# Output projection of a gated mix of attention and feed-forward: seven products for two tiles of results

## The chip, the cores and the metric

The kernel runs on one core of a Trainium2 chip. TensorE multiplies matrices (a stationary operand of 128x128 is loaded, then a moving one streams through), VectorE (DVE), ScalarE (ACT) and GpSimd (POOL) work element by element, SyncE (SP) issues the transfers. Results of TensorE land in PSUM, in eight banks of 512 f32 numbers per partition. Each engine runs its own list of instructions in order, and they wait for each other by semaphores. The metric is the device time of the whole program in microseconds.

## The reference

```python
def _A_ref(x, wq, wk, wv, wo, beta):      # 32 heads of 18, segments of 512 tokens
    ...                                   # local softmax and a memory of earlier segments
    return o @ wo                         # the output projection: [2048, 576] x [576, 576]

def _B_ref(x, w_gate, w_up, w_down):
    return (_gelu(x @ w_gate) * (x @ w_up)) @ w_down      # 576 -> 4608 -> 576

g = _sigmoid((x * gate_w).sum(-1, keepdims=True))
return g * _A_ref(x, ...) + (1 - g) * _B_ref(x, ...)
```

All arrays are f32. The output is [1, 2048, 576].

## The kernel before

Every f32 operand of a large product is scaled by a power of two and split in two f16 words, a high half (rounded) and a low half (what the rounding left). A product of two such operands takes three f16 products: high x high, high x low, low x high. A scale is made from a sum of squares, by a product with a matrix of ones (`sums`, L91, through `scale_sum`) and a few tiny operations of VectorE (L98 to L101). `low_x` (L175) makes the low half of x, `pair_high` and `pair_low` (L109, L112) the halves of a weight.

The program has three parts. First come the projections to q, k and v, with the memory of the attention (to 219.6 us). Then `step(v)` runs for v = 0 to 71, two steps for each of 36 slices of 128 hidden columns of the feed-forward part. A step makes gate and up for 1024 tokens (`product`, `rest`, `low_rests`; they already use a form with seven products for two by two blocks, whose sums of weights GpSimd makes), a share of the attention, and a share of the down projection of earlier slices (`chains`, `down`). The halves of the hidden values are made by `hidden` (VectorE, L1029) and `hidden_pair` (ScalarE L1033, GpSimd L1034). `end_pair` does this at the beginning of the next step for the products that a step left open. Third, behind the last step, come the last block of `down`, 16 tiles of 128 tokens with two halves of 288 columns each (32 chains of six products), and the output projection.

In the output projection the rows of the attention's result, tile t of 128 tokens, are loaded back and transposed by transfers (`turned(t)`, into `ot[t]`: four high tiles of 128 columns, four low ones, and one that holds both halves of the last 64 columns). W_o is loaded and squared by `finish(0)` and `finish(1)` behind steps 69 and 70, scaled by `finish(2)`, and its halves are made by `finish(3)` and `pair_low`. Each of 32 results (tile t, half n) takes 14 products (`chain_x`, L332 to L335): three for each of four tiles of columns and two for the last. VectorE then multiplies by the gate and adds to `acc` (L1327), and SP stores the tile.

The order is written by hand: within the schedule each of the four compute engines runs its instructions in the order in which the code issues them. What comes earlier in the code on an engine comes earlier in its list, also where its operands are late. Tiles come from pools with a fixed number of buffers: a new tile waits for the readers of the one whose buffer it takes. The tags that matter here are `pairg` (two, weights of gate and up), `x16` (four, halves of x), `raw` (three), the PSUM banks `dn` (two), `V`, `st` (two), `G`, `U` and `pv`.

## Time and profile before

| | us |
|---|---|
| median of 3 runs | 1586.41 (1586.34 to 1586.68) |
| the profiled execution | 1586.13 |
| its span in the trace | 1584.4 |
| TensorE busy | 1575.9 (99%) |
| VectorE, ScalarE, GpSimd busy | 1124.5, 1161.1, 1133.9 |
| last block of down, from the last product of step 71 | 1501.12 to 1526.18 |
| output projection on TensorE | 1526.18 to 1581.10 |

A row of a group names line, engine, operation, tile written and tiles read, shapes and count; behind the first bar stand busy us and the mean ns of one, behind the second the engine's idle time just before and what ended it. A row of the chain of waits has start, us and what ran. A row of the timeline is one or more instructions that follow each other, with start and us. A row of stretches gives busy us and instructions of each engine from one time to another, the granted TensorE clock (1.00 is full), the share of the transfer engines and GB/s.

### The profile page before, as it was taken

To read this page: it belongs to the slowest core of one execution; us is meant where nothing else is said; L and a number is where in the kernel's file an instruction comes from. 1 tells how busy PE (TensorE), PEld (TensorE's weight loads), DVE (VectorE), ACT (ScalarE), POOL (GpSimd) and SP (SyncE) were. 2 spreads that over 40 slices of the span, in tenths; PEclk is the share of its full clock that TensorE was granted. 3 is DMA by queue.
4 is the path that set the end of the run, shared out by engine and by line. 5 is a ranking of instruction groups with operands and counts; after the bars stand their busy time and mean duration, and the time that the engine had idled before them with its cause. 6 is when DMAs were issued, how large, how long until landed. Compare 5 with 4: busy or idle time off the path is not lost.

```text
span 1584.4 us, 32582 instructions
## 1 busy us (share of the span) xinstructions
PE 1575.9 (99%) x11912; PEld 940.2 (59%) x11912; DVE 1124.5 (71%) x2954; ACT 1161.1 (73%) x1976; POOL 1133.9 (72%) x1094
## 2 busy tenths in 40 slices
PE   9999999999999999999999999999999999999999
PEld 5666754555555555555555555555555555555577
DVE  6667784777777777767777777777777777776552
ACT  6666444888888888878888878888888888875300
POOL 2233756788888879898888888887979788887200
PEclk9999999999999999999999999999999999999999
DMA  6532442687878797888778889888898888863744
GB/s 232 208 120 90 140 136 75 104 128 127 134 134 135 127 152 125 138 127 140 130 126 131 135 133 140 135 141 145 126 143 129 136 132 136 133 115 54 175 106 123
DMA packets 472823, 209.87 MB, mean 132 GB/s; under 512 B 427688, under 2 KB 437160, under 8 KB 472152
## 3 DMA queue, kind: packets, MB, share of 16 engines
q1 hardware_dynamic: 472664, 207.80, 71.3%
q8 instruction: 93, 1.52, 0.4%
q14 instruction: 66, 0.54, 0.1%
HBM read 91.87 MB, written 27.26 MB: 75 GB/s over the span
## 4 chain that ended last, share of the span: by engine, by line
PE 95%; DVE 2%; ACT 1%; DMA 1%; issue 0%; SPq 0%; DVEq 0%
PE dn L1007 27%; PE U L1047 18%; PE V L1047 12%; PE G L1047 12%; PE pv L962 4%; PE st L332 3%; PE U L1054 2%; PE st L322 2%; PE dn L332 2%; PE G L322 1%; PE V L1059 1%; PE G L1059 1%; PE st L915 1%; PE G L1054 1%; PE V L1054 1%; PE U L322 1%
## 5 line engine op out<-in xcount | busy, mean ns | idle before, releaser
L942 POOL TENSOR_TENSOR ph<-pf,ph 128x512 f16<-128x512 f32 (+1 forms) x256 | 353.9, 1404 | 173.7 <-ACT ph L941 173.7
L1007 PE MATMUL dn<-paird,hh 128*128 128x288 f16 x3390 | 475.8, 286 | 0.8 <-DVE acc L1015 0.8
L1047 PEld LDWEIGHTS <-pairg 128*128 128x128 f16 x3024 | 285.4, 98 | 304.1 <-issue 17.8
L1007 PEld LDWEIGHTS <-hh 128*128 128x128 f16 x3456 | 332.2, 98 | 154.5 <-issue 19.1
L1015 DVE SCALAR_TENSOR_TENSOR acc<-dn,ev,acc 128x288 f32<-128x288 f32 x533 | 273.6, 514 | 53.2 <-PE dn L1007 43.0
L931 ACT ACTIVATE pf<-pf,mb,esc 128x512 f32<-128x512 f32 (+3 forms) x512 | 292.9, 642 | 7.0 <-POOL ph L942 0.4
L1047 PE MATMUL U<-xt,pairg 128*128 128x512 f16 x864 | 210.0, 379 | 0.0
L1047 PE MATMUL G<-x,pairg 128*128 128x512 f16 x864 | 209.9, 379 | 0.0
L1034 POOL TENSOR_TENSOR hh<-gl,hh 128x512 f16<-128x512 f32 x144 | 164.4, 1163 | 39.0 <-ACT hh L1033 39.0
L303 POOL TENSOR_TENSOR pairg<-raw,pairg 128x640 f16<-128x640 f32 (+2 forms) x144 | 174.2, 1233 | 5.1 <-ACT pairg L299 5.1
L299 ACT ACTIVATE pairg<-raw 128x640 f16<-128x640 f32 (+2 forms) x144 | 89.9, 650 | 113.2 <-POOL raw L293 65.2
L941 ACT ACTIVATE ph<-pf 128x512 f16<-128x512 f32 (+1 forms) x256 | 172.5, 721 | 0.0
L1188 DVE COPY gl<-U 128x512 f32<-128x512 f32 x72 | 49.8, 691 | 167.3 <-POOL hh L1034 150.3
L918 DVE CUSTOM_DVE_ANT_0 pf<-st,mask 128x512 f32<-128x512 f32 (+1 forms) x256 | 156.9, 613 | 0.0
L268 POOL TENSOR_SCALAR raw<-raw,sc 128x640 f32<-128x640 f32 x72 | 135.8, 1900 | 0.0
L1037 ACT ACTIVATE gl<-gl,sc 128x512 f32<-128x512 f32 x144 | 96.6, 715 | 42.7 <-DVE gl L1208 24.9
L918 DVE CUSTOM_DVE_ANT_0 pf<-dn,mask 128x256 f32<-128x256 f32 (+1 forms) x192 | 67.1, 375 | 82.8 <-PE dn L915 82.5
L1047 PE MATMUL V<-xt,pairg 128*128 128x512 f16 x432 | 105.7, 381 | 0.0
L1047 PE MATMUL U<-x,pairg 128*128 128x512 f16 x432 | 105.0, 379 | 0.0
L1047 PE MATMUL V<-x,pairg 128*128 128x512 f16 x432 | 104.8, 378 | 0.0
L1033 ACT ACTIVATE hh<-gl 128x512 f16<-128x512 f32 x144 | 82.6, 616 | 19.5 <-DVE gl L1029 19.4
L962 PEld LDWEIGHTS <-pt 128*128 128x128 f16 x2560 | 83.4, 96 | 6.3
(276 smaller groups left out, 2550.8 us busy)
## 6 DMA issues: line engine op xcount, KB each, us to landing
raw<-in_wgu_dram SPq DMA_DIRECT2D x36, 640.0 KB
rawd<-in_wd_dram SPq DMA_DIRECT2D x36, 288.0 KB
qt<-qk SPq DMA_DIRECT2D x132, 72.0 KB
kt<-qk SPq DMA_DIRECT2D x132, 72.0 KB
qk<-stage SPq DMA_DIRECT2D x36, 256.0 KB
qt<-qk SPq DMA_DIRECT2D x132, 36.0 KB
kt<-qk SPq DMA_DIRECT2D x132, 36.0 KB
vp<-vstage SPq DMA_DIRECT2D x16, 296.0 KB
```

The costliest lines, as they stand in the source:

```text
L268: pool.tensor_scalar(r, r, scl[f // 2][0][:, 0:1], None, OP.mult)
L303: pool.tensor_tensor(spot(f, *p, 1), raw_g[f][:, p[0] : p[1]], spot(f, *p, 0), OP.subtract)
L918: dve.tensor_tensor_reduce(prob[a][:, COL[qi] : COL[qi + 1]], out[qi], mask[:, L - (qi + 1) * P :], 1.0, -3e38, OP.add, OP.max, mx[a][:, q ...
L931: act.activation(r, r, AF.Exp, bias=b[:, qi : qi + 1], scale=esc[:, 0, c : c + 1])
L941: act.activation(h[:, 0, cols], p[:, cols], AF.Copy)
L942: pool.tensor_tensor(h[:, 1, cols], p[:, cols], h[:, 0, cols], OP.subtract)
L962: pe.matmul(ov, pr[:, 10 * i + COL[qi] // P + kb], v[:, 4 * e + kb, c0 : c0 + VC], start=kb == 0 and i == 0, stop=kb == qi and i == 1)
L1007: pe.matmul(o[:, :NH], hh[:, a, q * P : (q + 1) * P], w[:, b, n * NH : (n + 1) * NH], start=i == 0, stop=i == 5)
L1015: dve.scalar_tensor_tensor(av, o[:, :NH], ev, av, OP.mult, OP.add)
L1034: pool.tensor_tensor(hh[:, 1], t, hh[:, 0], OP.subtract)
L1037: act.activation(t, o, AF.Gelu_apprx_tanh, scale=scl[f // 2][0][:, 2 + c : 3 + c])
L1047: pe.matmul(o, w[:, i, (a + k) * P : (a + k + 1) * P], x[:, b + k], start=start and k == 0 and i == 0 and b == h, stop=k == 1 and i == 1, ...
```

## The change

Two result tiles x = 2u and y = 2u + 1 (pair u, of 0 to 7) are made together. Their four blocks over the first 512 columns (tile x or y, first or second 256 columns) are the blocks of a, W_o's four blocks those of b. Seven products of sums and differences of these blocks give the four blocks of results, and the last 64 columns go in plainly (`out_rest`). `sums_a(u)` makes the sums of a for a pair: two additions of high and low half back to f32 (L1334, on GpSimd, for pairs 3, 5 and 7 on VectorE), four sums (L1338 to L1341, GpSimd), their high halves (L1346, ScalarE) and low halves (L1347, GpSimd). `sum_w` (L1320), `high_w` (L1323) and `low_w` (L1326) do the like for W_o. `out_step(u, p)` issues product p of pair u and what VectorE does with it. Product 1 goes to a bank X, VectorE copies it to Y (L1385), and both go on as accumulators.

`finish(2)`, `sums_a(0)` and `finish(3)` are moved into the last step, before its last gate and up products. The hidden values that this step leaves open are no longer made at once behind t = 0 of the last block of down, but one behind t = 1 and one behind t = 2. W_o comes in three loads into `raw` tiles and is squared in three pieces, eleven tiles of rows are turned ahead in place of ten. In the first part `low_x(0, 1)` stands behind the scale of the q and k weights instead of before it.

```diff
--- before.py
+++ after.py
@@ -641,7 +641,6 @@
             vb = [bank("G"), bank("U"), bank("st", 2), bank("st", 2)]
             for q in range(4):
                 put_rows(0, q, 0, va[q], usc, 1.0)
-            low_x(0, 1)
...
@@ -671,6 +670,7 @@
                         turns.update(of=2)
                         scale_sum(0, wst[:, 10:19])
                         turns.update(of=3)
+                        low_x(0, 1)
                         later.pop(3)()
                         make_qk(0)
                         low_x(0, 2)
@@ -849,7 +849,8 @@
         zo = wts.tile([P, 2], F32, name="zo", tag="zo", bufs=1)
         dve.tensor_reduce(zo[:, 1:2], x2, AX.X, OP.max)
-        dve.tensor_tensor(zo[:, 0:1], wz[:, 1:2], zo[:, 1:2], OP.mult)
+        dve.tensor_scalar(zo[:, 0:1], wz[:, 1:2], zo[:, 1:2], 16.0, OP.mult, OP.mult)
         scale_of(3, zo[:, 0:1])
@@ -1239,6 +1240,10 @@
                 pair_rows(2 * k, 1)
                 turn_rows(2 * k)
             some(fb - 1, late[1:])
+            if v == 2 * NF - 1:
+                finish(2)
+                sums_a(0)
+                finish(3)
             if low is not None:
                 result_low(low)
             if on(k - 1):
@@ -1255,33 +1260,145 @@
             if k >= 0 and k % 4 == 0:
                 load_memory(k // 4)
-        wos, rows = {}, {}
-        ot = {}
+        ot, rows, sums_o, wo16 = {}, {}, {}, {}
         def turned(t):
             hf, r = divmod(t, 8)
             row = op_.tile([P, 9 * P], F16, name="orow", bufs=2)
             sp.dma_start(row, oas[hf][r * P : (r + 1) * P, :])
-            ot[t] = op_.tile([P, 9, P], F16, name="ot", bufs=10)
+            ot[t] = op_.tile([P, 9, P], F16, name="ot", bufs=11)
             sp.dma_start(ot[t], row, transpose=True)
+        B11, B21, B22, T1, T2, T3, T4, R1, R2, RD = 0, 2, 4, 6, 8, 10, 12, 14, 15, 16
...
         def finish(i):
             if i == 0:
-                for k in range(KT):
-                    rows[k] = op_.tile([P, D], F32, name="wor", bufs=5)
-                    sp.dma_start(rows[k], wo[:, k])
+                for k in range(3):
+                    r = raw_tile()
+                    n = 2 if k < 2 else 1
+                    sp.dma_start(r[:, : n * D], flat(wo[:, 2 * k : 2 * k + n]))
+                    rows[k] = r[:, : 2 * D].rearrange("p (k c) -> p k c", k=2) if k < 2 else r
             if i == 1:
-                for k in range(KT):
-                    wos[k] = op_.tile([P, 2, D], F16, name="wo", bufs=5)
-                    act.activation(wos[k][:, 1].bitcast(BF16), rows[k], AF.Square, accum_out=wst[:, k : k + 1])
+                wo16[0] = op_.tile([P, 2, 17, NH], F16, name="wo", bufs=1)
+                for k in range(3):
+                    r = flat(rows[k]) if k < 2 else rows[k][:, :D]
+                    junk = flat(wo16[0][:, k % 2]).bitcast(BF16)
+                    act.activation(junk[:, : r.shape[1]], r, AF.Square, accum_out=wst[:, k : k + 1])
             if i == 2:
-                scale_sum(2, wst[:, 0:5])
-                dve.tensor_scalar(gate[:, 2], gate[:, 0], wis[:, 2:3], wis[:, 3:4], OP.mult, OP.mult)
+                sq = wts.tile([P, 3], F32, name="sq4", tag="sq4", bufs=1)
+                dve.tensor_scalar(sq, wst[:, 0:3], 4.0, None, OP.mult)
+                scale_sum(2, sq)
             if i == 3:
-                for k in range(KT):
-                    pair_high(wos[k], rows[k], wsc[:, 2:3])
+                rows["t"] = flat(xt[0]).bitcast(F32)[:, : 8 * NH].rearrange("p (k c) -> p k c", k=8)
+                for k in range(3):
+                    r = flat(rows[k]) if k < 2 else rows[k][:, :D]
+                    act.activation(r, r, AF.Copy, scale=wsc[:, 2:3])
+                sum_w(T3)
+                sum_w(T1)
+                high_w(B11)
+                high_w(T3)
+        def sum_w(b):
+            x, y = {T1: (1, B11), T2: (B22, T1), T3: (B22, 1), T4: (B21, T2), RD: (R1, R2)}[b]
+            x, y = (rows[0][:, :, NH:] if c == 1 else words_of(c) for c in (x, y))
+            pool.tensor_tensor(words_of(b), x, y, OP.subtract)
+        def high_w(b):
+            act.activation(half_of(b, 0), words_of(b), AF.Copy)
+        def low_w(b):
+            pool.tensor_tensor(half_of(b, 1), words_of(b), half_of(b, 0), OP.subtract)
+        def sums_a(u):
+            w = flat(wts.tile([P, 2, GB * P], F16, name="pairg", tag="pairg", bufs=2)).bitcast(F32)
+            a, r = w[:, : 8 * P], w[:, 8 * P : 16 * P]
+            for i in range(2):
+                o = ot[2 * u + i]
+                (dve if u in (3, 5, 7) else pool).tensor_tensor(a[:, 4 * P * i : 4 * P * (i + 1)], flat(o[:, 0:4]),
+                                                               flat(o[:, 4:8]), OP.add)
+            a11, a12, a21, a22 = (a[:, 2 * P * i : 2 * P * (i + 1)] for i in range(4))
+            s1, s2, s3, s4 = (r[:, 2 * P * i : 2 * P * (i + 1)] for i in range(4))
+            pool.tensor_tensor(s3, a11, a21, OP.subtract)
+            pool.tensor_tensor(s1, a21, a22, OP.add)
+            pool.tensor_tensor(s2, s1, a11, OP.subtract)
+            pool.tensor_tensor(s4, a12, s2, OP.subtract)
+            if u % 2 == 0:
+                sums_o["x"] = flat(wts.tile([P, 9, L], F16, name="x16", tag="x16", bufs=4))
+            t = sums_o["x"][:, (u % 2) * 16 * P : (u % 2 + 1) * 16 * P]
+            sums_o[u] = t.rearrange("p (i b c) -> p i b c", i=2, b=8)
+            act.activation(t[:, : 8 * P], r, AF.Copy)
+            pool.tensor_tensor(t[:, 8 * P :], r, t[:, : 8 * P], OP.subtract)
+        def out_product(o, a, b, start=False):
+            w = wo16[0]
+            for k in range(2):
+                for i, j in ((0, 0), (0, 1), (1, 0)):
+                    pe.matmul(o[:, :NH], a(i, k), w[:, j, b + k], start=start and k == 0 and i == 0 and j == 0,
+                              stop=k == 1 and i == 1, skip_group_check=True)
+        def out_rest(o, t, b):
+            for j in range(2):
+                pe.matmul(o[:, :NH], ot[t][:, 8], wo16[0][:, j, b], start=False, stop=j == 1, skip_group_check=True)
+        def put_out(o, t, n):
+            av = acc[:, t, n * NH : (n + 1) * NH]
+            dve.scalar_tensor_tensor(av, o[:, :NH], gate[:, 2, t : t + 1], av, OP.mult, OP.add)
+        def store(t, n=None):
+            c = slice(0, D) if n is None else slice(n * NH, (n + 1) * NH)
+            sp.dma_start(out[t * P : (t + 1) * P, c], acc[:, t, c])
+        ob3 = {}
+        def out_step(u, p):
+            x, y = 2 * u, 2 * u + 1
+            S = lambda n: lambda i, k: sums_o[u][:, i, 2 * (n - 1) + k]
+            A = lambda t, k0: lambda i, k: ot[t][:, 4 * i + k0 + k]
+            if p == 7:
+                V = ob3[u, "V"] = bank("pv" if u % 2 else "V")
+                out_product(V, S(3), T3, True)
+                out_rest(V, y, R2)
+                put_out(V, y, 1)
+            if p == 1:
+                X, Y = bank("U" if u % 2 else "G"), bank("st", 2)
+                ob3[u, "X"], ob3[u, "Y"] = X, Y
+                out_product(X, A(x, 0), B11, True)
+                dve.tensor_copy(Y[:, :NH], X[:, :NH])
+            if p == 4:
+                V = ob3[u, "V"]
+                out_product(V, A(y, 2), T4)
+                out_rest(V, y, RD)
+                put_out(V, y, 0)
+            if p == 2:
+                X = ob3[u, "X"]
+                out_product(X, A(x, 2), B21)
+                out_rest(X, x, R1)
+                put_out(X, x, 0)
+            if p in (6, 5, 3):
+                Y = ob3[u, "Y"]
+                out_product(Y, S({6: 2, 5: 1, 3: 4}[p]), {6: T2, 5: T1, 3: B22}[p])
+                if p == 3:
+                    out_rest(Y, x, R2)
+                put_out(Y, *{6: (y, 0), 5: (y, 1), 3: (x, 1)}[p])
         LAG = 4
@@ -1306,29 +1423,56 @@
             fb = NB - 1
-            for t in range(turned_n, 10):
+            NT = 8
+            for t in range(turned_n, 11):
                 turned(t)
+            work = [lambda b=b: (high_w(b), low_w(b)) for b in (R2, T4, RD, B21, R1, T2, T1, B22)]
             for t in range(16):
                 for n in range(2):
                     down(fb, t, n)
-                if t == 0:
-                    end_pair()
                 if t in (1, 2):
-                    finish(1 + t)
-                if 4 <= t < 4 + KT:
-                    pair_low(wos[t - 4], rows[t - 4], wsc[:, 2:3])
-            for t in range(10, 16):
-                turned(t)
-            for t in range(16):
-                for n in range(2):
-                    o = bank("st", 2)
-                    chain_x(o[:, :NH], lambda i: ot[t][:, i], lambda k, b: wos[k][:, b, n * NH : (n + 1) * NH])
-                    av = acc[:, t, n * NH : (n + 1) * NH]
-                    dve.scalar_tensor_tensor(av, o[:, :NH], gate[:, 2, t : t + 1], av, OP.mult, OP.add)
-                    if t == 15:
-                        sp.dma_start(out[t * P :, n * NH : (n + 1) * NH], av)
-                if t < 15:
-                    sp.dma_start(out[t * P : (t + 1) * P, :], acc[:, t])
+                    f, c, o, g = ends.pop(0)
+                    hidden(f, c, o, g)
+                    hidden_pair(f, c, g)
+                if t == 3:
+                    low_w(T3)
+                    low_w(B11)
+                    sum_w(T2)
+                    sum_w(T4)
+                    sum_w(RD)
+                if t == 5:
+                    dve.tensor_scalar(gate[:, 2], gate[:, 0], wis[:, 2:3], wis[:, 3:4], OP.mult, OP.mult)
+                if t >= 4 and work:
+                    work.pop(0)()
+            for p in (7, 1, 4, 2):
+                out_step(0, p)
+            for u in range(NT):
+                if u + 1 < NT:
+                    sums_a(u + 1)
+                if u + 2 < NT:
+                    steps = (0, 6), (1, 7), (1, 1), (0, 5), (1, 4), (1, 2), (0, 3)
+                elif u + 1 < NT:
+                    steps = (0, 6), (1, 7), (1, 1), (0, 5), (1, 6), (0, 3)
+                else:
+                    steps = (0, 2), (0, 5), (0, 4), (0, 3)
+                for i, p in steps:
+                    out_step(u + i, p)
...
+                if u + 1 < NT:
+                    store(2 * u)
+                    store(2 * u + 1)
+                for t in (11 + 2 * u, 12 + 2 * u):
+                    if t < 16:
+                        turned(t)
```

TensorE's list gets 96 rows shorter, 48 weight loads and 48 products. Three places of the lists follow; the tile numbers are the program's own.

GpSimd (POOL) at the end of its list. Before, with `paird` the halves of the last down weights and `hh` those of the hidden values:

```order
L307 TENSOR_SCALAR rawd<-rawd,sc 128x576
L315 TENSOR_TENSOR paird<-rawd,paird 128x576
L1034 TENSOR_TENSOR hh_20725<-gl,hh_20725 128x512
L1034 TENSOR_TENSOR hh_20728<-gl,hh_20728 128x512
L1368 UNCONDITIONAL_BRANCH
```

Now, with `pairg` the f32 sums of pair 0, `x_20690` their halves, `xt_100` sums of W_o:

```order
L307 TENSOR_SCALAR rawd<-rawd,sc 128x576
L315 TENSOR_TENSOR paird<-rawd,paird 128x576
L1334 TENSOR_TENSOR pairg<-ot 128x512 x2
L1338 TENSOR_TENSOR pairg<-pairg 128x256
L1339 TENSOR_TENSOR pairg<-pairg 128x256
L1340 TENSOR_TENSOR pairg<-pairg 128x256
L1341 TENSOR_TENSOR pairg<-pairg 128x256
L1347 TENSOR_TENSOR x_20690<-pairg,x_20690 128x1024
L1320 TENSOR_TENSOR xt_100<-raw 128x576 x2
L1035 TENSOR_TENSOR hh_20763<-gl,hh_20763 128x512
L1035 TENSOR_TENSOR hh_20783<-gl,hh_20783 128x512
L1326 TENSOR_TENSOR wo<-xt_100,wo 128x576
```

The last hidden halves now stand behind the sums of pair 0 and two sums of W_o. Behind the last row come the other halves and sums of W_o (one more of L1326, three of L1320, eight of L1326), and then the sums of pairs 1 to 7.

VectorE (DVE) at the scale of W_o. Before:

```order
L1029 SCALAR_TENSOR_TENSOR gl<-U,sc,gl 128x512
L1015 SCALAR_TENSOR_TENSOR acc<-dn,ev,acc 128x288
L1015 SCALAR_TENSOR_TENSOR acc<-V,ev,acc 128x288
L105 TENSOR_REDUCE sv<-dn 128x1
L98 TENSOR_SCALAR wz<-sv 128x1
L77 TENSOR_SCALAR va<-wz 128x1
L78 TENSOR_SCALAR va<-va 128x1
L100 TENSOR_SCALAR wsc<-va 128x1
```

Now:

```order
L1216 TENSOR_TENSOR gl<-V,gl 128x512
L1016 SCALAR_TENSOR_TENSOR acc<-dn,ev,acc 128x288 x5
L1305 TENSOR_SCALAR sq_20671<-wst 128x3
L105 TENSOR_REDUCE sv<-dn 128x1
L98 TENSOR_SCALAR wz<-sv 128x1
L77 TENSOR_SCALAR va<-wz 128x1
L78 TENSOR_SCALAR va<-va 128x1
L100 TENSOR_SCALAR wsc<-va 128x1
```

The scale moved up into the last step, right behind the writes of its chains, and a new operation (L1305, called sq4 in the code) stands before its product.

VectorE in the output projection, from the last writes of pair 1 (bank st_21080) to the first of pairs 2 and 3 (st_21160, pv_21228); `ot_20712` and `ot_20716` are tiles 6 and 7:

```order
L1363 SCALAR_TENSOR_TENSOR acc_99<-V_21149,gate_78,acc_99 128x288
L1363 SCALAR_TENSOR_TENSOR acc_99<-G_21159,gate_78,acc_99 128x288
L1363 SCALAR_TENSOR_TENSOR acc_99<-st_21080,gate_78,acc_99 128x288
L1334 TENSOR_TENSOR pairg_21212<-ot_20712 128x512
L1334 TENSOR_TENSOR pairg_21212<-ot_20716 128x512
L1363 SCALAR_TENSOR_TENSOR acc_99<-st_21160,gate_78,acc_99 128x288
L1363 SCALAR_TENSOR_TENSOR acc_99<-pv_21228,gate_78,acc_99 128x288
L1385 COPY st_21239<-U_21238 128x288
```

The two additions of pair 3 are new there. They stand behind the write of pair 1's last product and before the first write of pair 2 in this loop; those of pairs 5 and 7 stand likewise two and four loops on.

18 lines of the change are left out of this document (added).

## The prediction

> **What bounds the kernel now.** I read the busy shares first, then the table of stretches, then the chain of waits over the last 100 us.
>
> ```profile
> PE 1575.9 (99%) x11912; PEld 940.2 (59%) x11912; DVE 1124.5 (71%) x2954; ACT 1161.1 (73%) x1976; POOL 1133.9 (72%) x1094
> ...
> 1500.00:1520.00 20.00, 19.16 (x154) 14.71 (x153) 17.71 (x39) 4.70 (x7) 2.27 (x2) 1.00 0.45 106
> 1520.00:1540.00 20.00, 20.00 (x166) 15.96 (x164) 8.47 (x18) 0.00 (x0) 0.00 (x0) 1.00 0.37 92
> 1540.00:1560.00 20.00, 20.00 (x166) 15.98 (x164) 6.15 (x12) 0.00 (x0) 0.00 (x0) 1.00 0.79 190
> 1560.00:1584.00 24.00, 21.06 (x172) 16.59 (x170) 6.73 (x13) 0.00 (x0) 0.00 (x0) 1.00 0.23 87
> ```
>
> The columns are TensorE, weight loads, VectorE, ScalarE, GpSimd, granted clock, DMA. TensorE is full from end to end. In the last 64 us ScalarE and GpSimd do nothing at all. The chain says what TensorE does there.
>
> ```profile
> 1500.80 0.32 PE G L1059
> 1501.12 0.84 PE V L1007 x6
> ...
> 1502.74 0.52 DVE acc L1015
> 1503.26 1.32 DVE gl L1029 x2
> ...
> 1507.49 0.90 PE dn L1007 x6
> ...
> 1526.18 1.47 PE st L332 x12
> 1527.65 0.12 PE st L334
> 1527.77 0.12 PE st L335
> ...
> 1581.10 0.52 DVE acc L1327
> ```
>
> The output projection runs from 1526.18 to 1581.10 without a hole: 54.92 us for 448 products, 0.1226 us each. It waits for nobody, so the 48 products that the change drops are worth their full price, unless the new operands come late. Ahead of it the last block of the down projection has its one hole: VectorE (1502.74 to 1507.4) holds the banks.
>
> **The change part by part.**
>
> *Products.* Per pair of result tiles 7 x 6 products and 4 rests of 2 make 50 in place of 56; over 8 pairs 400 in place of 448: 48 x 0.1226 = **-5.9 us**. A set of six takes 0.735, one with a rest 0.98, a pair 6.13.
>
> *What the sums cost on GpSimd.* The rows of such work, and those nearest to the new forms:
>
> ```profile
> L942 POOL TENSOR_TENSOR ph<-pf,ph 128x768 f16<-128x768 f32 x128 | 210.8, 1647 | 0.0
> L1034 POOL TENSOR_TENSOR hh<-gl,hh 128x512 f16<-128x512 f32 x144 | 164.4, 1163 | 39.0 <-ACT hh L1033 39.0
> L315 POOL TENSOR_TENSOR paird<-rawd,paird 128x576 f16<-128x576 f32 x36 | 46.2, 1285 | 6.3 <-ACT paird L311 6.3
> L303 POOL TENSOR_TENSOR pairg<-raw,pairg 128x384 f16<-128x384 f32 x36 | 33.7, 937 | 0.0
> L289 POOL TENSOR_TENSOR raw<-raw 128x256 f32<-128x256 f32 x36 | 26.2, 728 | 0.2
> L369 POOL TENSOR_TENSOR acc<-acc 128x1024 f32<-128x1024 f32 x2 | 4.7, 2354 | 2.4 <-DVE acc L360 2.4
> ...
> L170 ACT ACTIVATE x<-raw,xsc 128x1024 f16<-128x1024 f32 x8 | 9.0, 1138 | 1.5 <-DVE xsc L163 1.5
> ...
> L360 DVE TENSOR_TENSOR acc<-acc 128x1024 f32<-128x1024 f32 x5 | 6.1, 1220 | 0.0
> L481 DVE TENSOR_TENSOR phi<-phi,expm 128x512 f32<-128x512 f32 x1 | 0.7, 692 | 0.1
> L1327 DVE SCALAR_TENSOR_TENSOR acc<-st,gate,acc 128x288 f32<-128x288 f32 x32 | 16.6, 518 | 38.3 <-PE st L335 38.3
> ```
>
> For one pair: four sums of 256 numbers, 4 x 0.73 = 2.92. Then ScalarE's rounding of 1024, 1.14 and some 0.1 of handing over. Then GpSimd's subtraction of 1024 into f16: by 512 and 768 each 256 more cost 0.49, so 2.13. These three, 6.3 us, follow each other and cannot overlap, since each reads the one before. Ahead of them stand two additions of 512 f16 numbers into f32, which no row shows: at least as dear as 256 in f32 (0.73), at most 1.27 in f32 (a third of the way from 0.73 for 256 to 2.35 for 1024). I take 1.16, the row of the same length with one f16 operand. A pair wholly on GpSimd is then 2.3 + 6.3 + 0.1 = **8.7 us**, and TensorE uses up a pair in 6.13. GpSimd's idle tail doesn't help, if it cannot begin early.
>
> *When GpSimd can begin.* These are rows of the last step and behind it:
>
> ```profile
> 1490.83 1.28 POOL L315 TENSOR_TENSOR paird<-rawd,paird 128x576 f16<-128x576 f32 x1 [0.80 <-ACT paird L311]
> ...
> 1504.72 2.27 POOL L1034 TENSOR_TENSOR hh<-gl,hh 128x512 f16<-128x512 f32 x2 [12.61 <-ACT hh L1033]
> ...
> 1500.84 0.52 DVE L1015 SCALAR_TENSOR_TENSOR acc<-dn,ev,acc 128x288 f32<-128x288 f32 x1 [0.25 <-PE dn L1007]
> ...
> 1504.01 0.28 PE L91 MATMUL dn<-wst,ones 128*128 128x5 f32 x2
> ...
> 1505.34 0.15 DVE L105 TENSOR_REDUCE sv<-dn 128x1 f32<-128x5 f32 x1
> ...
> 1506.28 3.44 ACT L109 ACTIVATE wo<-wor,wsc 128x576 f16<-128x576 f32 x5 [0.98 <-DVE wsc L100]
> ```
>
> Pair 0's sums fall into the hole of 12.61 us from 1492.1, hidden. The weights' sums need the scale. Its product (L91) now stands right behind the last step's chains and needs sq4, which VectorE makes after the write of 1500.84 to 1501.36: TensorE waits about 0.8 us, to 1501.6. The scale follows 1.2 us later (from L105 to ScalarE's start 0.94 in the rows, and L91 itself), ScalarE's two multiplications of 1152 numbers end near 1505.7, and GpSimd starts. Its list then holds 4 sums of 576 in f32 (between 0.73 and 2.35: 1.4 each), one of 288 (0.8), the two hh of 1.16, 7 low halves of 576 (1.285) and 3 of 288 (0.77, from 384 less the slope to 512): 5.6 + 0.8 + 2.3 + 9.0 + 2.3 = 20.0 us, to **1525.7**. Only then come pair 1's sums, ready at 1534.4.
>
> *The down block* gains a little. In 1500.80 to 1526.18, 25.38 us, lie 192 products (23.5), 0.6 for L1059 and L91, and 1.3 of hole. Now: the 0.8 above, and no pile-up, as the two hidden products (1.32 in the chain) go one by one behind t = 1 and 2, with three banks. The hh for t = 8 are ready near 1511, three us early. So **-0.4**, and the projection begins at 1525.8.
>
> *The run of the projection.* Pair 0's first four sets take 30 products, to 1529.5; set 6, and at 1530.2 TensorE wants pair 1. Two products use the rounded half alone (0.25), then it waits for the low half at 1534.4: **4.0 us**. The rest of a loop is 5.15 us after the low half, to 1539.6. Pair 2 is ready 8.7 us after pair 1, at 1543.1: it is wanted 0.73 after 1539.6, less 0.25, a wait of **2.6**; the loop ends at 1548.3.
>
> Pair 3 is another matter. Its two additions are VectorE's, and there they stand behind the last write of the loop before, which needs that loop's last product. So nothing of pair 3 starts before 1548.3: the write 0.6, two additions of 0.65 (0.69 from the row; bounds 0.3, if halved by f16, and 1.22), then 6.3. Low half at 1556.5, wanted at 1549.0: with the 0.25, **7.3 us**. GpSimd stands idle for some seven of them. Queued behind TensorE's waiting weight load is the whole rest of the projection; behind that VectorE's writes, and behind these SP's stores and the row loads for tiles 11 to 15, which are wanted tens of us later.
>
> Pairs 4 and 6 repeat 2.6, pairs 5 and 7 repeat 7.3. Waits: 4.0 + 3 x 2.6 + 3 x 7.3 = **+33.7 us**. From pair 7's low half at 1601 there are 7.6 us of products left, to 1608.6, against 1581.10.
>
> *The prologue.* One low half of x goes behind the scale of the first weights.
>
> ```profile
> 20.80 2.48 DVE L175 SCALAR_TENSOR_TENSOR x<-raw,xsc,x 128x1024 f16<-128x1024 f32 x2
> 23.20 0.51 DVE L511 SCALAR_TENSOR_TENSOR vstage<-dn,usc,vstage 128x288 f16<-128x288 f32 x1
> ...
> 23.76 0.30 PEld L91 LDWEIGHTS dn<-wst,ones 128*128 128x128 f32 x2 [1.18 <-DVE vstage L511]
> ...
> 26.00 0.89 DVE L112 SCALAR_TENSOR_TENSOR wp<-acc,wsc,wp 128x640 f16<-128x640 f32 x1 [0.35 <-ACT wp L109]
> ```
>
> L511, which frees L91's bank, comes 1.24 earlier, so TensorE's 0.7 of waiting goes. L112, which the first projection's third product reads, then ends near 27.2 in place of 26.9, about when TensorE gets there: **-0.6**, bounds -0.7 and +0.5. The factor 16, three squares for five and three loads of W_o for five lie under TensorE's last steps: nothing; uncovered they'd cost their own 0.2 to 3 us.
>
> *Sum*: -5.9 - 0.4 - 0.6 + 33.7 = +26.8. The profiled execution took 1586.13 us (span 1584.4; the 1.7 around it and the last write and store stay). It lies 0.28 below the median of 1586.41. **1586.1 + 26.8 = 1613 us**, 1.7% slower.
>
> **A rule weighed.**
>
> ```profile
> PE G L614 <- POOL onesb L610: 1.2, 1, 1.2
> ```
>
> In the table of TensorE's waits this is the longest, and the clock is 1.00 in every stretch; 7 us of waiting this trace never had. The Trainium skill (TensorE: Matmul & The Clock Gate, Part 1: The HAM clock gate) says that TensorE's clock falls to half after an idle window of about 3.4 us and comes back after as long a busy one. No row of the trace of before can confirm it. By it each long wait would cost an estimated 1.7 us, three of four hidden in the 2.6 us that follow, and the time would be 1615.
>
> **The rivals.**
>
> *The clock falls in the long waits.* For it: waits of 4 and 7 us are new here. Against it: no row shows a lower clock. Suppose half the products behind a long wait run at half speed: 2.6 us more in a loop, just what the next pair's wait hides, but 3.8 of the 7.6 behind pair 7: 1617.
>
> *GpSimd's rate alone decides.* If the three pairs whose additions are VectorE's were not late, GpSimd would go 8.7, 6.3, 8.7 and so on from 1534.4, pair 7 at 1534.4 + 3 x 8.7 + 3 x 6.3 = 1579.4; plus 7.6 is 1587.0, 5.9 later than now, less 0.6: 1591. Against it: the place of L1334 in VectorE's list behind a write of the loop before.
>
> *Faster: the sums stay hidden.* If a pair took GpSimd under 6.1 us and VectorE's additions came a loop early, all waits would vanish and 1586.1 - 6.9 = 1579 be left. For it: GpSimd's and ScalarE's idle 64 us. Against it: four sums and a subtraction alone are 5.0, with rows of 36 and 128 instances; and even at half of every GpSimd duration the late additions would leave 0.6 + 1.3 + 1.5 + 1.2 + 1.1 - 1.0 = 4.7 us three times, more than the 6.9. It decides only where the additions are not late.
>
> **How the numbers follow.** Forecast 0.52, fallen clock 0.30, rate alone 0.07 (0.02 of it so cheap that nothing changes), hidden sums 0.05, and 0.06 for a loss beyond these. 0.2% (3 us) is what a measurement of this kernel can tell from no change: faster 0.05, same 0.02, slower 0.93. Range: eight unknown additions on GpSimd at -0.4 or +0.1 each (-3.4, +0.9), six on VectorE (-2.1, +3.4), GpSimd's list before pair 1 and the handings over (2 each way), the fallen clock +4. Not all at once: **1604 to 1621**.
>
> **What would show it.** Right: products at 0.12 us still, 400 of them; waits of TensorE at L1354 for ScalarE and GpSimd (L1346, L1347), longest at pairs 3, 5, 7; GpSimd idle before L1338 on VectorE's L1334, three times. Right in part: the 0.8 at L91 and no pile-up of L1030. Wrong: L1347 under 1 us, L1334 early, or no waits of TensorE behind 1526. A lower PEclk there would be the second rival.

## The result, and the profile after

The changed kernel takes **1614.79 us** (median of 5, 1612.85 to 1616.95) against 1586.34 (1585.51 to 1586.68) for the kernel before, measured beside it: the ratio is 1.0181, with an interval of 1.0166 to 1.0196. It is slower by 1.8%; 1613 was forecast. The profiled execution took 1612.85 us, its span is 1611.1.

The busy shares of the changed kernel, from its page, and its table of stretches (columns as before: TensorE, weight loads, VectorE, ScalarE, GpSimd, granted clock, DMA):

```profile
PE 1579.4 (98%) x11864; PEld 937.7 (58%) x11864; DVE 1137.5 (71%) x2980; ACT 1173.4 (73%) x1988; POOL 1202.7 (75%) x1159
...
1500.00:1520.00 20.00, 19.73 (x159) 15.53 (x160) 15.66 (x36) 9.56 (x15) 15.81 (x15) 1.00 0.43 92
1520.00:1540.00 20.00, 17.51 (x127) 12.68 (x125) 9.49 (x20) 2.11 (x2) 17.19 (x17) 0.91 0.24 60
1540.00:1560.00 20.00, 12.58 (x87) 8.84 (x87) 7.13 (x15) 1.53 (x2) 10.72 (x12) 0.83 0.48 130
1560.00:1580.00 20.00, 12.28 (x82) 8.35 (x81) 7.20 (x14) 1.64 (x2) 10.71 (x10) 0.85 0.13 48
1580.00:1600.00 20.00, 13.16 (x93) 9.29 (x92) 7.27 (x14) 2.11 (x2) 8.54 (x8) 0.84 0.16 60
```

There are 48 products fewer, and yet TensorE is busy 3.5 us longer than the 1575.9 of before. From 1540 us on it works 12 to 13 us of each 20, and it does so at a granted clock of 0.83 to 0.85, where before it stood at 1.00 in all stretches. So there are two things to explain: holes, and slow products. The table of TensorE's waits behind 1495 us names who ends the holes (total, times, longest, in us):

```profile
PE pv L1354 <- ACT x L1346: 16.5, 4, 5.3
PE pv L1354 <- POOL x L1347: 6.4, 4, 1.8
PE V L1354 <- POOL x L1347: 1.6, 2, 0.9
PE dn L91 <- DVE sq L1305: 0.7, 1, 0.7
```

Waiting for sums comes to 16.5 + 6.4 + 1.6 = 24.5 us. Bank pv belongs to pairs 1, 3, 5, 7, bank V to the even ones: 22.9 of the 24.5 lie at the odd pairs. Why those, GpSimd's rows tell (start, length, what; in brackets the idle time ahead and who ended it), with VectorE's two rows behind the three dots at the end:

```profile
1529.95 2.12 POOL L1347 TENSOR_TENSOR x<-pairg,x 128x1024 f16<-128x1024 f32 x1 [1.17 <-ACT x L1346]
1532.03 2.26 POOL L1334 TENSOR_TENSOR pairg<-ot 128x512 f32<-128x512 f16 x2
...
1538.55 2.13 POOL L1347 TENSOR_TENSOR x<-pairg,x 128x1024 f16<-128x1024 f32 x1 [1.17 <-ACT x L1346]
1547.89 0.72 POOL L1338 TENSOR_TENSOR pairg<-pairg 128x256 f32<-128x256 f32 x1 [7.21 <-DVE pairg L1334]
...
1552.06 2.12 POOL L1347 TENSOR_TENSOR x<-pairg,x 128x1024 f16<-128x1024 f32 x1 [1.17 <-ACT x L1346]
...
1569.99 0.72 POOL L1338 TENSOR_TENSOR pairg<-pairg 128x256 f32<-128x256 f32 x1 [7.21 <-DVE pairg L1334]
...
1592.09 0.72 POOL L1338 TENSOR_TENSOR pairg<-pairg 128x256 f32<-128x256 f32 x1 [7.21 <-DVE pairg L1334]
...
1546.09 0.52 DVE L1363 SCALAR_TENSOR_TENSOR acc<-st,gate,acc 128x288 f32<-128x288 f32 x1 [0.46 <-PE st L1359]
1546.52 1.28 DVE L1334 TENSOR_TENSOR pairg<-ot 128x512 f32<-128x512 f16 x2
```

A pair wholly on GpSimd goes from 1529.95 to 1538.55, low half to low half: 8.6 us. For pairs 3, 5 and 7 GpSimd stands idle for 7.21 us each time, until VectorE's two additions are there, and these begin right behind the write of the loop before. On TensorE's list the same place reads so:

```profile
1545.89 0.90 PE L1354 MATMUL st<-wo,x 128*128 128x288 f16 x6
1552.04 0.66 PE L1354 MATMUL pv<-wo,x 128*128 128x288 f16 x2 [5.25 <-ACT x L1346]
1554.24 1.14 PE L1354 MATMUL pv<-wo,x 128*128 128x288 f16 x4 [1.54 <-POOL x L1347]
...
1555.65 1.60 PE L1354 MATMUL U<-wo,ot 128*128 128x288 f16 x6
1557.08 0.90 PE L1354 MATMUL st<-wo,x 128*128 128x288 f16 x6
```

The wait is 5.25 us for the rounded half and 1.54 more for the low half. Behind it a set of six shows 1.60 us in place of 0.90, and from its start to the next set's 1.43 us pass in place of 0.74: its products run at about half the rate, from 1552.04, the end of the first wait, until 1557.08, then at the old one.

### The profile page after: what moved, and what is told of

The parts are those of the page before. It is cut to its first block, busy times and chain, and to the rows that moved or that the text cites. A ratio compares the mean times of both kernels' runs of the same rounds, so it can differ in the third digit from the quotient of the medians.

```text
span 1611.1 us, 32581 instructions
## 1 busy us (share of the span) xinstructions
PE 1579.4 (98%) x11864; PEld 937.7 (58%) x11864; DVE 1137.5 (71%) x2980; ACT 1173.4 (73%) x1988; POOL 1202.7 (75%) x1159
## 4 chain that ended last, share of the span: by engine, by line
PE 91%; POOL 4%; ACT 2%; DVE 2%; DMA 1%; issue 1%; SPq 0%; POOLq 0%; DVEq 0%; ACTq 0%
PE dn L1008 25%; PE U L1048 17%; PE V L1048 12%; PE G L1048 12%; PE pv L963 4%; PE U L1055 2%; PE st L322 2%; PE dn L332 2%; PE G L322 1%; PE V L1060 1%; PE G L1060 1%; PE st L916 1%; PE G L1055 1%; PE V L1055 1%; PE U L322 1%; PE dn L916 1%
## 5 line engine op out<-in xcount | busy, mean ns | idle before, releaser
L1048 PEld LDWEIGHTS <-pairg 128*128 128x128 f16 x3024 | 285.4, 98 | 304.1 <-issue 17.8
```

The lines of the kernel that those rows point to most:

```text
L1048: pe.matmul(o, w[:, i, (a + k) * P : (a + k + 1) * P], x[:, b + k], start=start and k == 0 and i == 0 and b == h, stop=k == 1 and i == 1, ...
```

## The experiments

All times below are medians, and each ratio is to the kernel before, run beside it (1585.69, 1585.82 and 1585.89 us in the three groups; it took 1586.34 beside the changed kernel, so differences to that one are good to some 0.7 us). The theory on trial is the forecast's: the loss comes from sums that are late, and they are late because VectorE's additions for pairs 3, 5 and 7 stand behind a write of the loop before. Rivals: GpSimd has too much to do; the new products are slower in themselves; the fallen clock costs the time.

**Without the sums.**

```diff
-                    sums_a(u + 1)
+                    sums_o[u + 1] = sums_o[0]
```

> The changed kernel without the sums of pairs 1 to 7: the projection reads pair 0's sums for every pair, so this part of the computation is left out; all 400 products, all writes and stores and the weights' sums stay. If the whole loss lies in waiting for the sums: no wait of TensorE in the projection, clock 1.00, TensorE ends near 1573.7: 1579 us, 0.4% below before (-5.9 for the products, -0.4 for the down block, -0.6 for the prologue). If the products of the new form are themselves slower, or its banks or stores hold TensorE: above 1586.

Measured: 1579.43 us, ratio 0.9961 (0.9947 to 0.9974). TensorE's only wait behind 1495 us, and two stretches of that run:

```profile
PE dn L91 <- DVE sq L1305: 0.7, 1, 0.7
...
1540.00:1560.00 20.00, 20.00 (x166) 15.97 (x164) 11.71 (x23) 0.00 (x0) 0.00 (x0) 1.00 0.48 147
```

This kernel leaves out the sums of seven pairs. The products of the new form, its banks, writes and stores cost nothing unforeseen, and the new products are not slow in themselves: without those sums the change would be worth 6.5 us. This also splits the profiled execution of the changed kernel. From this run's span, 1577.4, to 1611.1 there are 33.7 us; 24.5 of them are the waits above, and 9.2 are left. TensorE's list says where these lie: from start to start its products take some 7.5 us more than at 0.1226 us each, right behind the waits, and each of the ten waits costs 0.16 us beside what the table counts (together 9.1).

**VectorE's additions back on GpSimd.**

```diff
-                (dve if u in (3, 5, 7) else pool).tensor_tensor(...)
+                pool.tensor_tensor(...)
```

> The additions of pairs 3, 5 and 7 go from VectorE to GpSimd, so GpSimd gets 6.8 us more to do and nothing else changes. My theory (the additions are late where they stand on VectorE, GpSimd's rate comes second): GpSimd no longer stands idle for 7.2 us three times, pair after pair comes 8.6 us apart from 1532.1 on, pair 7 at 1583.7, and 7.6 of products and 5.3 behind them give 1597 us (up to 1599 if the clock falls). Rival (the amount of work on GpSimd alone decides): slower than the changed kernel by up to 6.8, 1613 to 1620. Rival (the products of the new form are slow in themselves): no change, about 1613.

Measured: 1597.04 us, ratio 1.0074 (1.0057 to 1.0091). GpSimd is given 6.8 us more to do, and the program gets 17.8 us shorter. That GpSimd's amount of work sets the time of the changed kernel is thereby out. What the slow products cost is asked further down. The pairs follow at 8.6 us and GpSimd no longer waits for VectorE; its additions for pair 3 start as soon as it is free:

```profile
1538.57 2.12 POOL L1346 TENSOR_TENSOR x<-pairg,x 128x1024 f16<-128x1024 f32 x1 [1.17 <-ACT x L1345]
1540.65 2.27 POOL L1334 TENSOR_TENSOR pairg<-ot 128x512 f32<-128x512 f16 x2
```

**The additions earlier on VectorE: three misses, and what was wrong with them.** The first try issued the additions of pairs 3, 5, 7 one loop earlier than the changed kernel does.

```diff
                     out_step(u + i, p)
+                    if (i, p) in ((0, 5), (1, 2)) and u + 2 in (3, 5, 7):
+                        add_a(u + 2, (i, p) == (1, 2), dve)
```

> The same additions of pairs 3, 5 and 7 on VectorE, issued one loop earlier; no instruction more or less. My theory: GpSimd's idle 7.2 us before these pairs go, pairs come 8.6 and 6.35 us apart by turns, pair 7 at 1532.1 + 3 x 8.6 + 3 x 6.35 = 1576.9, in all 1590 us. The rival that the amount of GpSimd's work decides: no change, about 1613, since that is the same. The rival that VectorE and GpSimd hinder each other when they work at the same time: GpSimd's rows L1338 to L1341 and L1347 get longer than 0.72 and 2.12, and the time stays above 1595.

Measured: 1610.26 us, ratio 1.0152. Two more in the same manner, first for all of pairs 1 to 7:

```diff
+                if 10 <= t < 14:
+                    add_a(1 + (t - 10) // 2, t % 2, dve)
...
-                    if (i, p) in ((0, 5), (1, 2)) and u + 2 in (3, 5, 7):
+                    if (i, p) in ((0, 5), (1, 2)) and 3 <= u + 2 < NT:
```

> The additions of pairs 1 to 7 all on VectorE, a loop or more earlier. GpSimd has 6.35 us for a pair and TensorE 6.13. My theory: pair 1 ready at 1529.8, pair 7 at 1567.9, in all 1581 us, faster than before by 0.3%. If GpSimd is hindered by VectorE (its rows longer), or VectorE's writes come late behind the additions: 1585 and more.

Then with one of the four sums and two low halves of W_o on VectorE as well:

```diff
+            if by is dve and i == 1:
+                w = added[u]
+                dve.tensor_tensor(w[:, 12 * P : 14 * P], w[:, : 2 * P], w[:, 4 * P : 6 * P], OP.subtract)
...
+                if t in (12, 14):
+                    low_w(T1 if t == 12 else B22, dve)
```

> As the run with all additions early on VectorE, and one of the four sums (L1338's, 256 numbers) and two low halves of W_o go to VectorE too: GpSimd has 5.6 us for a pair, less than TensorE's 6.13, and begins pair 1 2.6 us earlier. My theory: no wait of TensorE for sums is left, the 48 products less are worth their 5.9 us, and with the 1.2 that the changed kernel won ahead of the projection the time is 1579 us, 0.45% less than before. If something else than GpSimd's sums costs time in the new form (copies of X to Y, banks, the clock): 1582 and more.

Measured: 1621.29 us, ratio 1.0223, and 1621.47 us, ratio 1.0224. All three missed, by 20, 40 and 42 us. GpSimd's row of the first of the three shows that for pair 3 nothing had become earlier (for pairs 5 and 7 it idles 5.63 us in place of 7.21):

```profile
1547.67 0.72 POOL L1347 TENSOR_TENSOR pairg<-pairg 128x256 f32<-128x256 f32 x1 [7.30 <-DVE pairg L1335]
```

In loop u, sets 5 and 2 come behind product 7 of pair u + 1, and that product waits for the sums of its own pair. An addition behind their writes is therefore still tied to the sums of the pair just ahead, and with pairs 3 to 7 all so tied GpSimd idles 5.6 to 8.4 us ahead of each of them in the second run. The place, not the number of the loop, was the error, and it was mine. Next, then, the additions ahead of that product, right behind set 6:

```diff
+                    if (i, p) == (0, 6) and u + 2 in (3, 5, 7):
+                        for j in range(2):
+                            add_a(u + 2, j, dve)
```

> As the changed kernel, but the two additions of pairs 3, 5 and 7, still on VectorE, are issued two loops before their pair is used, right behind set 6 and so ahead of product 7 of the pair between (the first try put them behind that product's write, which itself waits for sums). Theory (only the place of the additions makes them late): pair 1 is ready at 1532.1 as in the changed kernel, the pairs then follow at 8.6 and 6.35 by turns, pair 7 at 1532.1 + 3 x 8.6 + 3 x 6.35 = 1577.0, plus 7.6 of products and 5.3 behind them: 1590 us, no GpSimd idle of 7 us before L1338's counterpart, TensorE's waits 1 to 3 us each. If VectorE's additions hinder GpSimd as in the earlier runs (0.44 us for each of six): up to 1593. Rival (an addition on VectorE costs its pair the time wherever it stands): above 1603, with the 7 us idle rows still there.

Measured: 1593.83 us, ratio 1.0048 (1.0034 to 1.0061): 21 us less than the changed kernel, by the place of six instructions alone. The rest to 1590 is in these rows of GpSimd, and of VectorE behind them:

```profile
1538.54 2.12 POOL L1356 TENSOR_TENSOR x<-pairg,x 128x1024 f16<-128x1024 f32 x1 [1.17 <-ACT x L1355]
1541.89 0.73 POOL L1347 TENSOR_TENSOR pairg<-pairg 128x256 f32<-128x256 f32 x1 [1.23 <-DVE pairg L1335]
...
1538.63 3.18 DVE L1335 TENSOR_TENSOR pairg<-ot 128x512 f32<-128x512 f16 x2
```

Two additions that took 1.28 us in the changed kernel take 3.18. They start 0.09 after a GpSimd instruction of 2.12 and end 1.15 after its end, about as if they had stood still until then. GpSimd then waits 1.23 for them, three times: 3.7 us, and 1590 + 3.7 is what was measured.

**All additions on VectorE, in the right place.**

```diff
-                    if (i, p) == (0, 6) and u + 2 in (3, 5, 7):
+                    if (i, p) == (0, 6) and 3 <= u + 2 < NT:
```

> As the run before, but the additions of all pairs 1 to 7 are on VectorE, those of pairs 1 and 2 in the last block of the down projection, the others two loops ahead, behind set 6. GpSimd then has 6.3 us for a pair against TensorE's 6.13. Theory without hindrance between the engines: pair 1 ready at 1529.8, pair 7 at 1529.8 + 6 x 6.35 = 1567.9, which is at about TensorE's own pace: 1579 to 1581 us. With hindrance (each of VectorE's additions makes a GpSimd row 0.44 us longer and is itself 0.9 longer): 7.2 a pair, pair 7 at 1573, and 7.6 + 5.3 more: 1586 us. Rival (lateness has another cause than the place): 1610 or more.

Measured: 1589.74 us, ratio 1.0023 (1.0014 to 1.0032), 3.7 above the dearer of the two cases. GpSimd idles for 1.23 us here too, for each of pairs 4 to 7. To see whether that was once more the place, the additions went half a loop earlier:

```diff
-                    if (i, p) == (0, 6) and 3 <= u + 2 < NT:
+                    if (i, p) == (1, 4) and u + 3 < NT:
                         for j in range(2):
-                            add_a(u + 2, j, dve)
+                            add_a(u + 3, j, dve)
```

> As the run with all additions of pairs 1 to 7 on VectorE, but those of pairs 3 to 7 three loops ahead, behind product 4 of the second pair of that loop, half a loop earlier than before. There GpSimd stood idle for 1.23 us a pair, waiting for the additions. Theory (that idle time is again the place): it vanishes, pairs follow at 6.3, pair 1 ready at 1531.6, pair 7 at 1569.6, and 7.6 + 5.3 more: 1582.5 us; if an addition at the same time as a GpSimd row costs that row 0.44, as in some rows seen: up to 1587. Rival (the additions' own length on VectorE, 2.1 for two, sets the period): 1589 to 1590 again.

Measured: 1586.71 us, ratio 1.0005 (0.9996 to 1.0014), the upper end of the first theory. GpSimd's groups behind 1523 us (busy, mean ns, and idle time ahead):

```profile
L1356 POOL TENSOR_TENSOR x<-pairg,x 128x1024 f16<-128x1024 f32 x7 | 16.9, 2408 | 8.2 <-ACT x L1355 8.2
...
L1347 POOL TENSOR_TENSOR pairg<-pairg 128x256 f32<-128x256 f32 x7 | 5.5, 788 | 1.9 <-DVE pairg L1335 1.9
```

The idle time is down to 1.9 us for seven pairs, but the low half now takes 2.41 in the mean in place of 2.12. The place was a part of it; what is left fits the second theory, that the two engines hinder each other, and this at both places tried.

**The hindrance by itself.** The kernel with all additions on GpSimd, with VectorE kept busy by work that nobody reads:

```diff
+                if u <= 3:
+                    dve.tensor_tensor(z, flat(o[:, 0:4]), flat(o[:, 4:8]), OP.add)
+                else:
+                    dve.tensor_copy(z, flat(o[:, 0:4]))
```

> As the run with all additions on GpSimd (1597.0), with work on VectorE that nobody reads, three operations behind writes of each of pairs 1 to 6: for pairs 1 to 3 an addition of two 128x512 f16 operands from SBUF, for pairs 4 to 6 a copy of one such operand, both into PSUM. Theory (VectorE and GpSimd get in each other's way at SBUF when VectorE reads two operands there): in the stretch of pairs 1 to 3 the additions take 0.9 to 1.7 us each in place of 0.65 and some GpSimd rows 0.4 more than elsewhere, pairs follow at 9 to 10 us; in that of pairs 4 to 6 nothing changes, 8.6 a pair: 1598 to 1601. Rival (the longer rows seen had another cause): GpSimd's rows and the period are the same in both stretches, 1597, additions 0.65.

Measured once: 1603.08 us against 1597.04 without that work, 2 us above the upper end of what was expected; the rows decide here, not the time. The two kinds on VectorE (shortest, median and longest in ns, first and last start), and rows of GpSimd in the time of the one and of the other:

```profile
L1373 DVE TENSOR_TENSOR dn<-ot x15: 683/793/2520, 1535.8 to 1569.0; 128x512 f32<-128x512 f16 x15
L1375 DVE CAST dn<-ot x13: 676/684/686, 1567.0 to 1586.5; 128x512 f32<-128x512 f16 x13
...
1554.38 1.17 POOL L1338 TENSOR_TENSOR pairg<-pairg 128x256 f32<-128x256 f32 x1
1555.63 1.05 POOL L1339 TENSOR_TENSOR pairg<-pairg 128x256 f32<-128x256 f32 x1
...
1573.94 0.73 POOL L1338 TENSOR_TENSOR pairg<-pairg 128x256 f32<-128x256 f32 x1
```

Thirteen copies of one operand take 0.68 us each, all alike, and GpSimd's row beside them keeps its 0.73. Fifteen additions of two operands take 0.68 to 2.52, and GpSimd's rows beside them 1.05 and 1.17. So the two-operand form on VectorE and GpSimd's work delay each other, and the one-operand form does not.

**The clock.** Forty products that nobody reads ahead of product 7 of pairs 3, 5, 7 fill most of the long waits:

```diff
+                if u in (3, 5, 7):
+                    o = bank("dn", 2)
+                    for _ in range(40):
+                        pe.matmul(o[:, :NH], ot[2 * u - 2][:, 8], wo16[0][:, 0, B11], start=True, stop=True)
```

> The changed kernel with 40 more products (128x288, into a bank nobody reads) ahead of product 7 of pairs 3, 5 and 7: 4.9 us of work that fills most of each wait of 7 us. Nothing else differs. If TensorE's idle time is what lets its clock fall, the granted clock stays at 1.00 behind 1525, no product of the projection takes double, the even pairs wait about 2.5 us again instead of 0.6 to 0.9, the end behind pair 7's low half takes 7.6 in place of 9.15, and the time is 1.5 us below the changed kernel's (about 1611 to 1613), with less spread between executions. If the clock falls for another reason, it shows 0.85 here too and the time is that of the changed kernel or above.

Measured: 1615.5 us (1611.60 to 1617.43), ratio 1.0180. The stretches of the profiled execution, which was the one of 1611.60:

```profile
1520.00:1540.00 20.00, 17.40 (x128) 12.63 (x125) 9.78 (x20) 2.11 (x2) 17.20 (x17) 0.91 0.26 60
1540.00:1560.00 20.00, 17.08 (x137) 13.22 (x138) 7.76 (x16) 1.47 (x2) 10.78 (x12) 1.00 0.51 134
1560.00:1580.00 20.00, 15.73 (x125) 11.68 (x124) 7.07 (x15) 1.70 (x2) 10.66 (x10) 1.00 0.12 45
```

Where the waits were filled the clock is 1.00, and that execution is 1.25 us below the changed kernel's profiled one, as expected. But the other three took 3.5 to 5.8 us more, and no less than the changed kernel, so the smaller spread that was expected did not come. What was left unfilled are waits of 2.1 to 2.5 us, ahead of every pair but the second. So these were filled too:

```diff
-                if u in (3, 5, 7):
+                if u:
                     o = bank("dn", 2)
-                    for _ in range(40):
+                    for _ in range(56 if u in (3, 5, 7) else 18):
```

> As the run with filled waits, but more of them: 56 unread products ahead of product 7 of pairs 3, 5, 7 (6.9 us) and 18 ahead of that of pairs 1, 2, 4, 6 (2.2 us), so that no wait of over 0.6 us is left. Question: why three of four executions of the run with filled waits took 3.5 to 5.8 us more than its profiled one. Theory (the clock also falls, in some executions, behind the even pairs' waits of 2.5 us, where nothing hides it, 1.5 us each time): with these filled too the clock is 1.00 in every execution, and all take 1611 to 1612.5, within 1.5 us of each other. Rival (the spread has another cause, in the memory traffic or in GpSimd): median 1615 again, spread 4 us or more.

Measured: 1611.28 us, 1611.02 to 1612.01, ratio 1.0164 (1.0150 to 1.0178). The same stretches, and what is left of the waits:

```profile
1520.00:1540.00 20.00, 19.54 (x159) 15.09 (x157) 9.60 (x19) 2.11 (x2) 17.20 (x17) 1.00 0.36 84
1540.00:1560.00 20.00, 19.54 (x159) 15.30 (x159) 7.92 (x16) 2.04 (x2) 10.21 (x12) 1.00 0.50 110
...
PE pv L1354 <- POOL x L1347: 1.5, 4, 0.5
```

With TensorE kept at work all five executions agree within 1.0 us, all of them below the fastest of the changed kernel (1612.85). So the clock falls because TensorE stands idle, and TensorE's idle time is what made the executions of the changed kernel differ by 4 us. That the fall of the clock is the link is likely and not shown for each execution: in the run before, the fastest has a mean granted clock of 0.999 and the others 0.996 to 0.997, but of the changed kernel's, 0.993 stands beside 1612.85 and beside 1614.90 too. That waits of 2.5 us in all can bring the clock down, the 0.91 of the run before shows, since only pair 1's waits of 0.7 and 1.8 lie ahead of it. With all waits filled the median is 3.5 us below the changed kernel's: this is an estimate of what the slow products cost, against the 17.8 and 21 us that moving the additions was worth.

**A version that beats both.** Where GpSimd takes 8.6 us for a pair and TensorE 6.13, two plain pairs among six of the new form give GpSimd its time. Their plain sets stand between those of the others.

```diff
+        FORM = (0, 2, 3, 5, 6, 7)
...
+            run((0, 7), (0, 1), (0, 4), (0, 2), (0, 6), ("c", 2, 0), (0, 5), ("c", 2, 1), (0, 3))
+            done(0)
+            sums_a(5)
+            run(("c", 3, 0), ("c", 3, 1))
...
+            run((2, 7), (2, 1), (2, 4), (2, 2), (2, 6), ("c", 8, 0), (2, 5), ("c", 8, 1), (2, 3))
```

> A version that keeps TensorE from waiting: the form with seven products for pairs 0, 2, 3, 5, 6, 7 only, all additions on GpSimd; pairs 1 and 4 (tiles 2, 3, 8, 9) with the plain 14 products for a half tile, put between the sets of the others so that GpSimd's 8.6 us for each of five pairs are covered; one more block of W_o (B12) is rounded for it. Products dropped: 6 x 6 = 36, -4.4 us; the prologue and the down block as in the changed kernel, -1 to -2. Theory: pairs 2, 3, 5, 6, 7 ready at 1533, 1541.6, 1550.2, 1558.8, 1567.4, each before it is wanted; no wait over 0.5 us, clock 1.00; TensorE ends near 1574.8: 1580 us, 0.3 to 0.4% below before. If the form's price lies elsewhere than in the late sums (slower products, the one more block, the stores): 1586 or above.

Measured: 1581.41 us (1580.87 to 1582.02), ratio 0.9969 (0.9958 to 0.9981): 4.4 us faster than the kernel before, 33 faster than the changed one. Its rows: a stretch with TensorE full, two low halves, and the only wait of TensorE behind 1495 us.

```profile
1540.00:1560.00 20.00, 20.00 (x165) 15.88 (x163) 9.79 (x20) 2.61 (x3) 16.62 (x16) 1.00 0.72 192
...
1531.97 2.12 POOL L1352 TENSOR_TENSOR x<-pairg,x 128x1024 f16<-128x1024 f32 x1 [1.17 <-ACT x L1351]
1540.57 2.13 POOL L1352 TENSOR_TENSOR x<-pairg,x 128x1024 f16<-128x1024 f32 x1 [1.17 <-ACT x L1351]
...
PE dn L91 <- DVE sq L1307: 0.7, 1, 0.7
```

GpSimd runs at the same 8.6 us a pair as in the slow kernels, and nothing waits for it.

## Why the prediction was right, point by point

*The products and the down block.* -5.9, -0.4 and -0.6 make -6.9; the run without the sums is 6.5 us below before, its span 7.0. The wait at L91 was forecast as 0.8 and is 0.7. From the end of the last step's chains to the projection there are 25.0 us (1499.6 to 1524.60) in place of 25.38: the -0.4.

*The prologue.* TensorE's wait at L91 is gone, as forecast. TensorE's timeline in the kernel before:

```profile
7.65 0.72 PE L531 MATMUL dn<-acc,raw 128*128 128x288 f32 x2 [0.75 <-DMA acc<-in_wv_dram]
...
23.77 0.39 PE L91 MATMUL dn<-wst,ones 128*128 128x9 f32 x2 [0.72 <-DVE vstage L511]
...
27.81 2.76 PE L322 MATMUL G<-x,wp 128*128 128x512 f16 x12
```

And in the changed one:

```profile
22.29 0.29 PE L91 MATMUL dn<-wst,ones 128*128 128x9 f32 x2
...
26.22 2.76 PE L322 MATMUL G<-x,wp 128*128 128x512 f16 x12
```

The first projection (L322) begins 1.6 us earlier and not 0.6. But 0.75 of this is a wait for a DMA that the profiled execution of before has, and no other trace of this case. The edit was not run alone, so its own share is read, not shown.

*GpSimd's list.* It ends at 1523.42, 1525.7 was forecast: its start was 1.6 earlier (1504.11), of which 1.2 is the whole program's lead, and the list itself took 19.3 in place of 20.0. Pair 1's low half is ready at 1532.07 and not 1534.4. So the first term was mis-sized: 4.0 forecast, 0.7 + 1.8 measured (what three times 5.25 and 1.54 leave of the 16.5 and 6.4 of the table of waits).

*The additions.* 1.16 was taken for GpSimd, which no row showed; two in a row take 2.26, so 1.13 each. On VectorE 0.65 was taken, and two take 1.28 in the changed kernel, where GpSimd stands still meanwhile. This was luck in one point: next to work on GpSimd one such row takes up to 2.6.

*The pace of two pairs.* 8.7 + 5.15 + 0.6 + 1.3 + 6.3, with 0.1 for handing over, gave 22.2 us from odd pair to odd pair. Measured: GpSimd's rows behind its three waits start at 1547.89, 1569.99 and 1592.09, so 22.1. This is the step on which the forecast stood, and moving VectorE's six additions to GpSimd (-17.8) and then to another place (-21) shows that it is the cause and not an accompaniment. The forecast was right here in the mechanism.

*What failed: "products at 0.12 us still".* The clock fell behind each long wait, which is the second rival's sign, given 0.30. The terms of the waits came out smaller for it, since a slow product fills a wait: 5.25 + 1.54 for the odd pairs in place of 7.3, 1.6 for all three even ones in place of 7.8 (at a clock of 1.00, in the run with the long waits filled, pairs 4 and 6 wait 0.35 + 1.78 each, so 0.5 of each 2.6 was a matter of size). Together 24.5 of waiting and 9.2 of slow work and ends of waits stand where 33.7 of waiting was forecast. That both sums are 33.7 is chance, but that slow products and waits make up for each other is not: when pair 7's low half is ready hangs on GpSimd, VectorE and the last product of a loop, and slow products that end before TensorE's next wait cost nothing. In the profiled execution the fall costs what lies behind pair 7's low half. TensorE's first products there and its last two, in the changed kernel:

```profile
1598.44 1.14 PE L1354 MATMUL pv<-wo,x 128*128 128x288 f16 x4 [1.54 <-POOL x L1347]
...
1607.29 0.41 PE L1359 MATMUL st<-wo,ot 128*128 128x288 f16 x2
```

And in the run with all waits filled:

```profile
1597.98 0.67 PE L1354 MATMUL pv<-wo,x 128*128 128x288 f16 x4 [0.36 <-POOL x L1347]
...
1605.38 0.41 PE L1359 MATMUL st<-wo,ot 128*128 128x288 f16 x2
```

That is 8.85 us against 7.40: 1.45 for the clock. In the median it costs more, 1614.8 against 1611.3; where, no trace shows. The rival's 1617 put 3.8 us behind pair 7, which was too dear for this execution.

That the profiled execution comes within 0.2 us of 1613 is therefore in part luck: pair 7's low half is ready 2.6 us earlier than forecast (1598.38 and not 1601.0; 0.6 of it was forecast for the prologue by itself), and the products behind it take 1.45 us longer than at the full clock. This execution is also the fastest of the five; the median lies 1.8 us above the forecast.

The Trainium skill (TensorE: Matmul & The Clock Gate, Part 1: The HAM clock gate) had the clock at half after an idle window of about 3.4 us, and by it the forecast weighed an estimate of 1.7 us at the end and 1615. The trace agrees: about half rate, 1.45 us at the end. In one point it differs: ahead of pair 1 TensorE idles only 0.7 and 1.8 us, with two products between, and the granted clock of that stretch still fell to 0.91. The same part of the Trainium skill also says that the window runs freely, so that the same kernel meets it at another point each time; a spread of 4 us that vanishes when TensorE is kept busy fits this.

*The other rivals.* "GpSimd's rate alone", 1591, is what the run with VectorE's additions in another place was to show: 1593.8, the difference being the hindrance. "Hidden sums", 1579: with the plain pairs between it is 1581.4, and 1579.4 without sums at all.

## What to carry to other kernels

Before work is shifted to an idle engine, look at what stands ahead of it in that engine's list: an instruction that needs nothing but early data is as late as the write in front of it, and two engines that take turns this way each look idle. Where a helper engine is slower than the one it feeds, feed less through it: six of eight pairs gained where eight of eight lost.

## What the runs showed of the hardware that was not expected

VectorE and GpSimd stand in each other's way when VectorE reads two operands from SBUF: 0.68 us became up to 2.6 when a GpSimd instruction of 2.12 had just begun, and GpSimd's 0.72 became 1.05 to 1.17. A one-operand copy of the same size did neither. The Trainium skill (SBUF — State Buffer, Who interferes with whom) says that the two engines share a pair of ports as an exclusive lock, and that a VectorE instruction with two SBUF inputs contends with a GpSimd instruction that reads SBUF. The rows agree: the two additions of 3.18 us ended 1.15 us after GpSimd's instruction, and alone they take 1.28. In the run with the additions half a loop earlier the price is 0.8 us a pair: five pairs take from 1531.50 to 1566.83, 7.1 each, where GpSimd's and ScalarE's own rows come to 6.3.

Waits of 2.5 us in all were enough to bring the clock down in some executions and not in others. TensorE waits 0.7 and 1.8 us ahead of pair 1 in the changed kernel, in the run with the additions of pairs 3, 5 and 7 behind set 6 and in the one with VectorE kept busy; the granted clock from 1520 to 1540 us is 0.91 in the profiled execution of the first and 1.00 in those of the other two. The changed kernel and the one with its long waits filled spread over 4.1 and 5.8 us, and over 1.0 us once all waits were filled. Why others with waits spread less, the run with all additions on GpSimd over 1.3 us, stays open.
